# Row maxima by an operation that also copies the scores: a threshold attention with a gated MLP on one core

## The chip, the cores and the metric

The kernel runs on one core of a Trainium2 chip. The metric is device time in microseconds; smaller is better. TensorE (PE) multiplies and writes PSUM; VectorE (DVE) and ScalarE (ACT) read PSUM and SBUF; GpSimd (POOL) reads SBUF only; SyncE (SP) issues most of the transfers. Each engine works through its own instructions strictly in the order in which they stand, and waits on semaphores for the others.

## The reference

The inputs are q, k and v of 8 batches, 8 heads, 576 rows and 64 columns, a threshold `tau` of 0.02, and the weights of a gated MLP.

```python
scale = 1.0 / np.sqrt(q.shape[-1])
scores = scale * np.matmul(q, k.transpose(0, 1, 3, 2))
thresh = np.max(scores, axis=-1, keepdims=True) - tau
scores = np.where(scores >= thresh, scores, -1000000000.0)
scores = scores - np.max(scores, axis=-1, keepdims=True)
attn = np.exp(scores)
attn = attn / (np.sum(attn, axis=-1, keepdims=True) + 1e-09)
x = np.matmul(attn, v)                       # heads side by side: (8, 576, 512)

h = np.maximum(x @ w_in, 0.0)                # 512 -> 1024
u, v = h[..., :512], h[..., 512:]
v_n = (v - mean(v)) / np.sqrt(var(v) + 1e-06)
v_s = np.einsum('ts,bsd->btd', w_spatial, v_n) + b_spatial[None, :, None]
out = (u * v_s) @ w_out
```

So every row of scores needs its maximum before anything else can be done with it: only the scores within `tau` of it survive, and those are weighted by their exponentials.

## The kernel before, in words

The heads are taken in pairs, 32 of them. A step `g` is 128 query rows of a pair against all 576 keys, 144 steps in all, 18 to a batch. Its scores, 576 columns for each of the two heads, lie in one of two PSUM buffers of three banks (`s_ring`), at columns 96 and 864, so that both heads share the middle bank.

A step runs as follows, with the letters by which the lists name its parts:

- `S`, `G`, `Y`: PE computes the scores (line 816). `G` is an empty instruction on some other engine that keeps two matmuls from the shared bank at one time.
- `M` (`top`, line 850): VectorE takes the maxima of both heads in one reduction over 1152 columns and writes their negatives into the shared bank of the same PSUM buffer.
- `B` (`shift`, line 856): VectorE makes of the two numbers the bias `negm` (threshold minus maximum), a tiny operation.
- `E`, `F` (`spread`, lines 871 and 874): ScalarE reads the scores of one head from PSUM and writes them, shifted, to SBUF, into one of three buffers `e`. After `F` the PSUM buffer is free for step g+2.
- A step is of one of two kinds (table `WAYS`, the same in both kernels). In the 96 steps of kind `a`, ScalarE's `E` and `F` are a leaky rectifier that drives all scores under the threshold far down, and `Z` (line 909) takes the exponential of 1152 columns into the half-precision buffer `p`. In the 48 of kind `n`, `E` and `F` take the exponential at once, in half precision, and VectorE makes a mask of it (`C`, line 893) and applies it (`A`, line 902).
- `T`: a transfer turns `p` into `pT`. `P`, `i`, `p`: PE multiplies by v with a column of ones, VectorE takes the reciprocals of the sums (line 531) and scales (line 534).

The MLP of a batch runs one to two batches behind its attention: `v`/`bv`, `n`, `k`, `bs`, `ba`, `N` (second half of the first product, its statistics and normalization), `u`/`eu` (first half), `s`/`es` (product with the spatial weights, then the gate on VectorE, line 752), `o`/`eo` (the output). `Q..`/`q..`/`kd` turn q and k on PE. The evictions from PSUM run on ScalarE, or with a `d` before their name on VectorE.

What runs when is written out by hand as `ORDER`, a list of such names for each of the eight batches, and `LAST`, for what follows: the numbers behind a colon say by how many batches a part lags. The program issues the parts in the order of the list, and each engine takes its own from that.

Of the kernel before, what the change touches and what calls it, by code (L numbers as in the profile page):

```python
# [34 lines left out]
(  # L35
# [18 lines left out]
(  # L54
# [130 lines left out]
def kernel(  # L185
# [17 lines left out]
    nc = tc.nc  # L203
# [592 lines left out]
    def on_act(g):  # L796

        return way(g) in "anrs"
# [445 lines left out]
```

## Time and profile before

| what | value |
|---|---|
| three timed runs | 436.28, 437.15 and 436.65 us, median 436.65 |
| profiled execution | span 433.6 us, first to last instruction; the page has no other time for it, and the median is 3.0 us above the span |
| TensorE clock granted | 1.00 |
| matmul / weight load busy | 407.3 us (94%) / 253.7 us (58%) |
| VectorE busy | 374.6 us (86%), 681 instructions |
| ScalarE busy | 383.9 us (89%), 587 instructions |
| GpSimd busy | 167.5 us (39%) |
| 144 row maxima (line 850) | 196.1 us of VectorE, from 7.5 us to 396.4 us (their starts) |
| 288 `E` and `F` (lines 871, 874) | 66.8 + 133.1 us of ScalarE |

A busy time is the time in which at least one instruction of the engine was in work; rows of one engine can overlap a little. A row of the groups reads: line, engine, operation, output and input with their shapes, count, busy time, mean of one in ns, then the idle time in front of them and what ended it. A row of the engines in order of time begins with its start and its length in us. A row of the stretches has the stretch, its length, and then the busy time of PE, weight load, VectorE, ScalarE and GpSimd in it.

### The profile page before, as it was taken

The numbers are of one execution on the slowest core, as the hardware profiler recorded it, in microseconds if no ns is written. First come the engines' busy times: TensorE is split into PE (matmuls) and PEld (weight loads), VectorE is DVE, ScalarE is ACT, GpSimd is POOL, SyncE is SP. The second block draws the span as 40 slices with busy tenths as digits, with TensorE's granted clock in tenths as the row PEclk, the third lists the DMA queues.
The fourth block names the chain that finished last, engine by engine and source line by source line (L and its number), as shares of the span: only waits on it lengthen the run. The fifth ranks groups of instructions, "written<-read, shape, count | busy, mean of one in ns | idle before, by whom it ended". The sixth has DMA issues, their size and how long they took to land.

```text
span 433.6 us, 12917 instructions
## 1 busy us (share of the span) xinstructions
PE 407.3 (94%) x5028; PEld 253.7 (58%) x5028; DVE 374.6 (86%) x681; ACT 383.9 (89%) x587; POOL 167.5 (39%) x374
## 2 busy tenths in 40 slices
PE   7678879989999999998999999999999999999995
PEld 4446655565755666574665656555666656564642
DVE  6999989898989889987889988988999999998652
ACT  4999989999999988998988999999999989999262
POOL 1253525682335611545143713356114630264020
PEclk9999999999999999999999999999999999999999
DMA  7999999999899998999979999999999999889923
GB/s 195 224 237 232 246 247 221 194 212 197 226 241 212 246 208 183 218 184 178 254 139 250 216 159 248 233 209 205 232 209 232 181 232 194 172 124 193 164 68 118
DMA packets 224700, 88.15 MB, mean 203 GB/s; under 512 B 195648, under 2 KB 220352, under 8 KB 224640
## 3 DMA queue, kind: packets, MB, share of 16 engines
q1 hardware_dynamic: 224192, 86.75, 99.7%
q8 instruction: 39, 0.64, 0.6%
q10 hardware_dynamic: 368, 0.33, 0.2%
q0 software_dynamic: 80, 0.26, 0.2%
q14 instruction: 21, 0.17, 0.2%
HBM read 32.79 MB, written 9.44 MB: 97 GB/s over the span
## 4 chain that ended last, share of the span: by engine, by line
PE 64%; ACT 13%; DVE 8%; DMA 6%; issue 4%; POOL 3%; SPq 0%; ACTq 0%; DVEq 0%; POOLq 0%
PE s L816 26%; ACT e L874 6%; PE f L738 6%; DVE s L850 5%; PE f L496 5%; PE f L709 5%; PE f L434 4%; PE f L642 4%; PE f L767 4%; DMA pT<-p 3%; ACT p L909 2%; DMA xT<-xn 2%; ACT e L871 2%; PE f L491 2%; PE f L627 1%
## 5 line engine op out<-in xcount | busy, mean ns | idle before, releaser
L850 DVE TENSOR_REDUCE s<-s 128x2 f32<-128x1152 f32 x144 | 196.1, 1362 | 21.3 <-PE s L816 18.0
L816 PE MATMUL s<-qkT 64*64 64x160 f32 (+1 forms) x2304 | 171.4, 415 | 12.6 <-ACT e L874 6.6
L816 PEld LDWEIGHTS s<-qkT 64*64 64x64 f32 x2304 | 106.5, 131 | 71.3 <-ACT e L874 18.8
L874 ACT ACTIVATE e<-s,negm 128x576 f32<-128x576 f32 x192 | 133.1, 744 | 9.6 <-DVE negm L856 7.0
L909 ACT ACTIVATE p<-e 128x1152 f16<-128x1152 f32 x96 | 111.6, 1173 | 0.7 <-PE s L816 0.2
L871 ACT ACTIVATE e<-s,negm 128x576 f16<-128x576 f32 x96 | 66.8, 746 | 5.0 <-DVE negm L856 2.9
L320 POOL CAST v<-vl 128x512 bf16<-128x512 f32 x32 | 20.2, 631 | 77.0 <-PE s L816 65.7
L496 PE MATMUL f<-v,pT 128*128 128x65 bf16 x984 | 44.4, 194 | 0.0
L496 PEld LDWEIGHTS <-pT 128*128 128x128 f16 x1024 | 41.8, 98 | 2.2 <-issue 0.2
L293 POOL COPY qn<-ql 128x512 f32<-128x512 f32 x31 | 20.4, 659 | 49.9 <-PE s L816 47.5
L902 DVE TENSOR_TENSOR p<-e 128x576 int32<-128x576 int32 x48 | 37.2, 778 | 0.4 <-PE s L816 0.2
L738 PE MATMUL f<-wsT,vn 128*128 128x512 bf16 x135 | 33.0, 380 | 0.0
L491 PE MATMUL f<-v,pT 128*128 128x130 bf16 x123 | 27.3, 222 | 3.6 <-DMA pT<-p 3.5
L709 PE MATMUL f<-xT,w_in 128*128 128x512 bf16 x116 | 29.7, 380 | 0.5 <-ACT qkT L414 0.3
L694 POOL TENSOR_SCALAR vn<-vrel,rs,nm 128x512 bf16<-128x512 f32 (+1 forms) x35 | 28.1, 801 | 3.6
L642 PE MATMUL f<-w_in,xT 128*128 128x512 bf16 x112 | 27.9, 380 | 0.3 <-DMA xT<-xn 0.3
L446 POOL COPY qkT<-qkT 64x64 f32<-64x64 f32 x32 | 9.5, 296 | 44.8 <-PE s L816 17.6
L534 DVE TENSOR_TENSOR xn<-f,r 128x384 bf16<-128x384 f32 x46 | 24.9, 551 | 1.3 <-PE s L816 0.8
L856 DVE TENSOR_SCALAR negm<-s 128x2 f32<-128x2 f32 x144 | 22.2, 154 | 4.0 <-PE s L816 1.5
L767 PE MATMUL f<-w_o,gT 128*128 128x512 bf16 x100 | 25.4, 379 | 0.1
L893 DVE TENSOR_SCALAR e<-e 128x1152 uint16<-128x1152 f16 x48 | 23.0, 478 | 0.1
L687 POOL TENSOR_TENSOR rs<-rs,mhalf 128x1 f32<-128x1 f32 (+1 forms) x35 | 21.2, 607 | 2.9
(171 smaller groups left out, 531.4 us busy)
## 6 DMA issues: line engine op xcount, KB each, us to landing
vl<-in_v_dram SPq DMA_DIRECT2D x16, 512.0 KB, 5.3
ql<-in_q_dram SPq DMA_DIRECT2D x15, 512.0 KB, 4.6
kl<-in_k_dram SPq DMA_DIRECT2D x15, 512.0 KB, 5.3
out_dram<-oo SPq DMA_DIRECT2D x12, 512.0 KB, 3.7
pT<-p SPq DMA_TRANSPOSE x141, 4.6
uT<-in_moe_w_in_dram SPq DMA_DIRECT2D x3, 512.0 KB, 5.1
uT<-in_moe_w_spatial_dram SPq DMA_DIRECT2D x2, 576.0 KB, 4.4
vx<-in_v_dram SPq DMA_DIRECT2D x16, 64.0 KB, 4.3
```

What stands on the lines that cost most here:

```text
L491: nc.tensor.matmul(out=t[:, at:at + 130], lhsT=pt[:, 4, rows], rhs=vt[:, 4:6, :].rearrange("p b d -> p (b d)"), start=True, stop=False)
L496: nc.tensor.matmul(out=t[:, at + 65 * h:at + 65 * h + 65], lhsT=pt[:, 5 * h + j, rows], rhs=vt[:, 6 * h + j, :], start=False, stop=(h == 1 ...
L642: nc.tensor.matmul(out=t, lhsT=x_of(b, f, slice(c * P, (c + 1) * P)), rhs=w_in[:, f, 512:1024], start=(f == 0), stop=(f == 3))
L709: nc.tensor.matmul(out=t, lhsT=w_in[:, m, f * P:(f + 1) * P], rhs=x_of(b, m, slice(0, 512)), start=(m == 0), stop=(m == 3))
L738: nc.tensor.matmul(out=t, lhsT=vn[:, c, f * P:(f + 1) * P], rhs=wsT[:, c, 0:512], start=(c == 0), stop=(c == 4))
L767: nc.tensor.matmul(out=t[:n], lhsT=gs[b][:, f, c * P:c * P + n], rhs=w_o[:, f, :], start=(f == 0), stop=(f == 3))
L816: made.append(nc.tensor.matmul(out=s_ring[g % 2][halves[k], at[h] + lo:at[h] + hi], lhsT=qks[n][halves[h], 0, m:m + 64], rhs=qks[n][halves ...
L850: nc.vector.tensor_reduce(out=nm[:, heads], in_=view(s_ring[g % 2], at[h0], dims), axis=AX.X, op=ALU.max, negate=True)
L871: nc.scalar.activation(out=half_e(g)[0][:, S * h:S * h + S], in_=s, func=ACT.Exp, bias=bias_, scale=scale if steps[g][1] == 4 else 1.0)
L874: nc.scalar.activation(out=e, in_=s, func=ACT.Prelu, bias=bias_, scale=scale if steps[g][1] == 4 else 1.0, alpha=1e30)
L902: nc.vector.tensor_tensor(out=numerators(g).bitcast(I32), in0=e.bitcast(I32), in1=kept.bitcast(I32), op=ALU.bitwise_and)
L909: nc.scalar.activation(out=numerators(g), in_=e_ring[g % 3].rearrange("p h s -> p (h s)"), func=ACT.Exp)
```

## The change

`M` becomes two operations, one for each head. Each reads 576 scores from PSUM, adds a column of zeros that is read 576 times over, writes the sum, which is the scores themselves, into the step's `e` buffer in SBUF, and keeps the largest of them, which goes to a small tile `peak` in SBUF. `B` reads `peak`, with the sign turned, since the old reduction gave the negative. `E` and `F` read the `e` buffer and write into the same buffer, in place. In the steps of kind `n`, where they write half precision, the result of a head lies in the first half of that head's own row, and the mask in its second half; the views in `C` and `A` become three-dimensional for that. A column `zero` is filled once. All eight lists and the first two of `LAST` are new, with no count of any part changed; some evictions have changed between VectorE and ScalarE.

```diff
@@ ORDER, one list of eight @@
-    "S0:0 G0:0 Y0:0 s0:2 OUT3:3 eu0:2 A15:1 E17:1 sq2:0 F17:1 S1:0 T13:1 M0:0 G1:0 Y1:0 s1:2 Z16:1 C17:1 L6:0 "
...
+    "S0:0 A15:1 aG0:0 Y0:0 QR1:0 M17:1 P100:1 P101:1 F16:1 qr1:0 E16:1 Z16:1 M0:0 P102:1 s0:2 i10:1 S1:0 "
...
+    zero = const.tile([P, 1], F32, name="zero")
...
-    negm = {}
+    negm, peak = {}, {}
 
     def top(g, heads=slice(0, 2)):
 
-        if on_act(g):
-            nm = s_ring[g % 2][:, 704:706]
-        elif g in negm:
-            nm = negm[g]
-        else:
-            nm = negm[g] = small.tile([P, 2], F32, name="negm")
-        h0, n = heads.start, heads.stop - heads.start
-        dims = [[at[1] - at[0], n], [1, S]] if n > 1 else [[1, S]]
-        nc.vector.tensor_reduce(out=nm[:, heads], in_=view(s_ring[g % 2], at[h0], dims), axis=AX.X,
-                                op=ALU.max, negate=True)
+        if g not in peak:
+            peak[g] = small.tile([P, 2], F32, name="peak")
+        for h in range(heads.start, heads.stop):
+            nc.vector.tensor_tensor_reduce(
+                out=e_ring[g % 3][:, h, :], in0=view(s_ring[g % 2], at[h], [[1, S]]),
+                in1=zero.broadcast_to([P, S]), scale=1.0, scalar=float("-inf"),
+                op0=ALU.add, op1=ALU.max, accum_out=peak[g][:, h:h + 1])
 
     def shift(g):
 
         nm = negm[g] = small.tile([P, 2], F32, name="negm")
-        nc.vector.tensor_scalar(out=nm, in0=s_ring[g % 2][:, 704:706],
-                                scalar1=scale if steps[g][1] == 4 else 1.0,
+        nc.vector.tensor_scalar(out=nm, in0=peak[g],
+                                scalar1=-(scale if steps[g][1] == 4 else 1.0),
                                 scalar2=float(tau) + (0.0 if way(g) == "a" else half_step),
                                 op0=ALU.mult, op1=ALU.add)
 
     def half_e(g):
 
-        t = e_ring[g % 3].rearrange("p h s -> p (h s)").bitcast(F16)
-        return t[:, 0:1152], t[:, 1152:2304]
+        t = e_ring[g % 3].bitcast(F16)
+        return t[:, :, 0:S], t[:, :, S:2 * S]
 
     def spread(g, h):
 
-        s = view(s_ring[g % 2], at[h], [[1, S]])
+        s = e_ring[g % 3][:, h, :]
...
+        nc.vector.memset(zero, 0.0)
```

What this makes of the instructions on each engine is shown at three places. First VectorE, inside a batch in the middle of the run, where nearly all of its work is of this kind. (`s_94` and `s_95` are the two PSUM buffers; `e_103` to `e_105`, after the change `e_104` to `e_106`, the three SBUF buffers; the names in brackets are the semaphores that an instruction waits for, by the engine or transfer that raises them.) Before:

```order
L850 TENSOR_REDUCE s_94<-s_94 128x2 [waits PE_49,Activation_49]
L902 TENSOR_TENSOR p_113<-e_105 128x576 [waits DMAHW3_49,DVE_49]
L856 TENSOR_SCALAR negm<-s_94 128x2 [waits DVE_49]
L850 TENSOR_REDUCE s_95<-s_95 128x2 [waits PE_49,Activation_49]
L893 TENSOR_SCALAR e_104<-e_104 128x1152
L856 TENSOR_SCALAR negm<-s_95 128x2 [waits DVE_49]
L902 TENSOR_TENSOR p_115<-e_104 128x576 [waits DMAHW1_49,DVE_49]
```

and with the change, two steps as well:

```order
L848 ISA e_105,peak<-s_94,zero 128x576 [waits PE_49,Activation_49]
L848 ISA peak 128x1
L848 ISA e_105,peak<-s_94,zero 128x576
L848 ISA peak 128x1
L856 TENSOR_SCALAR negm<-peak 128x2 [waits DVE_49]
L848 ISA e_106,peak<-s_95,zero 128x576 [waits PE_49]
L848 ISA peak 128x1
L848 ISA e_106,peak<-s_95,zero 128x576
L848 ISA peak 128x1
L755 TENSOR_TENSOR gT<-f,uT 128x512 [waits PE_49]
L856 TENSOR_SCALAR negm<-peak 128x2 [waits DVE_49]
```

One reduction has become four instructions: for each head the main one and a second, of one column, that puts out `peak`. The first of them now also writes `e`, and the wait for ScalarE (`Activation`) there is for the step that used this `e` buffer before.

Second TensorE, at the scores of one step in the same batch. Before:

```order
L816 MATMUL s_95<-qkT 64x160 [waits Activation_49]
L816 MATMUL s_95<-qkT 64x160
L816 MATMUL s_95<-qkT 64x416 x4
L816 MATMUL s_95<-qkT 64x160 [waits Pool_sequencer_49]
L816 MATMUL s_95<-qkT 64x160
```

and with the change:

```order
L819 MATMUL s_94<-qkT 64x160 [waits DVE_49]
L819 MATMUL s_94<-qkT 64x160
L819 MATMUL s_94<-qkT 64x416 x4
L819 MATMUL s_94<-qkT 64x160 [waits Pool_sequencer_49]
L819 MATMUL s_94<-qkT 64x160
```

The matmuls are the same. The first of them waited for ScalarE to give the PSUM buffer back and now waits for VectorE.

Third ScalarE in the same batch. Before:

```order
L874 ACTIVATE e_103<-s_94,negm 128x576 [waits DVE_49,Activation_49]
L874 ACTIVATE e_103<-s_94,negm 128x576
L412 ACTIVATE uT<-f 128x512 [waits PE_49]
L874 ACTIVATE e_104<-s_95,negm 128x576 [waits DVE_49]
L874 ACTIVATE e_104<-s_95,negm 128x576
L909 ACTIVATE p_111<-e_105 128x1152 [waits DMAHW1_49]
```

and with the change:

```order
L874 ACTIVATE e_105<-e_105,negm 128x576 [waits DVE_49]
L874 ACTIVATE e_105<-e_105,negm 128x576
L874 ACTIVATE e_106<-e_106,negm 128x576 [waits DVE_49]
L909 ACTIVATE p_111<-e_105 128x1152 [waits DMAHW2_49,Activation_49]
L874 ACTIVATE e_106<-e_106,negm 128x576
L657 ACTIVATE vrel<-f 128x512 [waits PE_49]
```

The two activations of a step now read the buffer that they write.

More of the change, by code (lines that the diff above doesn't have):

```diff
@@ L20 @@
 ORDER = [(
[14 rows of a table removed]
-(
[18 rows of a table removed]
-(
[18 rows of a table removed]
-(
[17 rows of a table removed]
-(
[17 rows of a table removed]
-(
[17 rows of a table removed]
-(
[17 rows of a table removed]
-(
[16 rows of a table removed]
[12 rows of a table added]
+(
[19 rows of a table added]
+(
[17 rows of a table added]
+(
[18 rows of a table added]
+(
[17 rows of a table added]
+(
[18 rows of a table added]
+(
[17 rows of a table added]
+(
[16 rows of a table added]
 LAST = [(
-    "C15:1 es1:2 OUT3:3 A15:1 E17:1 T13:1 s3:2 "),
-(
[3 rows of a table removed]
+    "u3:2 eu3:2 E15:1 s0:2 s1:2 es0:2 T11:1 T9:1 C15:1 T12:1 T7:1 OUT4:3 A15:1 T13:1 E17:1 s3:2 es1:2 OUT3:3 "
+    "F17:1 "),
+(
[4 rows of a table added]
 (
@@ L861, in half_e @@
     def half_e(g):
-        t = e_ring[g % 3].rearrange("p h s -> p (h s)").bitcast(F16)
-        return t[:, 0:1152], t[:, 1152:2304]
+        t = e_ring[g % 3].bitcast(F16)
+        return t[:, :, 0:S], t[:, :, S:2 * S]
     def spread(g, h):
-        s = view(s_ring[g % 2], at[h], [[1, S]])
+        s = e_ring[g % 3][:, h, :]
         e, bias_ = e_ring[g % 3][:, h, :], negm[g][:, h:h + 1]
         if way(g) in "nrs":
-            nc.scalar.activation(out=half_e(g)[0][:, S * h:S * h + S], in_=s, func=ACT.Exp,
+            nc.scalar.activation(out=half_e(g)[0][:, h, :], in_=s, func=ACT.Exp,
                                  bias=bias_, scale=scale if steps[g][1] == 4 else 1.0)
@@ L901, in pick @@
         if way(g) == "n":
-            nc.vector.tensor_tensor(out=numerators(g).bitcast(I32), in0=e.bitcast(I32),
+            nc.vector.tensor_tensor(out=numerators(g).rearrange("p (h s) -> p h s", h=2).bitcast(I32), in0=e.bitcast(I32),
                                     in1=kept.bitcast(I32), op=ALU.bitwise_and)
         else:
-            nc.gpsimd.tensor_tensor(out=numerators(g), in0=e, in1=kept, op=ALU.mult)
+            nc.gpsimd.tensor_tensor(out=numerators(g).rearrange("p (h s) -> p h s", h=2), in0=e, in1=kept, op=ALU.mult)
     def exps(g):
```

273 rows, old and new, of tables (LAST, ORDER) are left out of this document.

## Prediction

> **What bounds the kernel now.** I read the page's first part, then its chain, then the stretches, then the groups by form, and last the engines in order of time. The page says that TensorE is the fullest, but that two others stand close behind it:
>
> ```profile
> PE 407.3 (94%) x5028; PEld 253.7 (58%) x5028; DVE 374.6 (86%) x681; ACT 383.9 (89%) x587; POOL 167.5 (39%) x374
> PE 64%; ACT 13%; DVE 8%; DMA 6%; issue 4%; POOL 3%; SPq 0%; ACTq 0%; DVEq 0%; POOLq 0%
> ```
>
> Those are means over unlike stages. The row maxima run from 7.5 us to the end of the last one at 397.8 us; the view of stretches, cut there and at 60 us (columns: PE, weight load, DVE, ACT, POOL, then clock and DMA), gives
>
> ```profile
> 7.50:60.00 52.50, 40.53 (x591) 28.02 (x589) 49.05 (x77) 49.25 (x71) 19.98 (x42) 1.00 1.15 232
> 60.00:397.80 337.80, 330.16 (x4091) 206.16 (x4092) 302.45 (x533) 316.14 (x483) 142.68 (x319) 1.00 1.04 208
> 110.00:397.80 287.80, 283.69 (x3522) 176.60 (x3519) 258.88 (x457) 269.68 (x411) 115.62 (x262) 1.00 1.03 206
> 397.80:433.60 35.80, 30.73 (x316) 16.68 (x314) 18.98 (x49) 15.93 (x30) 3.31 (x5) 1.00 0.55 125
> ```
>
> The reader is to see two regimes. In the ramp (first row) there is hardly any gMLP work for TensorE yet: PE is busy 77% of it, VectorE 93.4% and ScalarE 93.8%, so there those two set the pace. From 60 us on PE takes over: 97.7% there, 98.6% from 110 us, with VectorE at 90% and ScalarE at 94%. The granted clock is 1.00 in every row. In the last 35.8 us no row maximum is left, and the order of instructions after the last scores has the same rows on PE in both kernels, so I leave that tail as it is.
>
> What PE waits for at the scores, and what VectorE waits for there, the view of waits says (us in total, times, longest):
>
> ```profile
> DVE s L850 <- PE s L816: 18.0, 43, 0.9
> PE s L816 <- ACT e L874: 6.6, 13, 0.9
> PE s L816 <- ACT e L871: 3.9, 10, 0.7
> ```
>
> PE itself loses 6.6 + 3.9 = 10.5 us because a PSUM buffer of scores is given back only when ScalarE has read it. This is what the change takes away; more than 10.5 us cannot come of that directly.
>
> **The change, part by part.** First VectorE. The rows that price it, from the groups by form:
>
> ```profile
> L850 DVE TENSOR_REDUCE s<-s 128x2 f32<-128x1152 f32 x144 | 196.1, 1362 | 21.3 <-PE s L816 18.0 <-PE f L496 0.8 <-ACT vrel L654 0.6
> L856 DVE TENSOR_SCALAR negm<-s 128x2 f32<-128x2 f32 x144 | 22.2, 154 | 4.0 <-PE s L816 1.5
> L752 DVE TENSOR_TENSOR gT<-f,uT 128x512 bf16<-128x512 f32 x27 | 18.4, 685 | 2.1 <-PE s L816 1.4 <-PE f L738 0.4
> L534 DVE TENSOR_TENSOR xn<-f,r 128x384 bf16<-128x384 f32 x46 | 24.9, 551 | 1.3 <-PE s L816 0.8
> ```
>
> A two-input operation with one input in PSUM takes 551 ns for 384 columns and 685 for 512, so (685 - 551)/128 = 1.05 ns a column, and 685 + 64 x 1.05 = 752 ns for the 576 columns of one head. Rows overlap, though, and what counts is from start to start. VectorE in order of time:
>
> ```profile
> 100.16 0.16 DVE L856 TENSOR_SCALAR negm<-s 128x2 f32<-128x2 f32 x1
> 100.24 0.68 DVE L752 TENSOR_TENSOR gT<-f,uT 128x512 bf16<-128x512 f32 x1
> 100.84 0.28 DVE L410 COPY qkT<-f 128x128 f32<-128x128 f32 x1
> 106.05 1.37 DVE L850 TENSOR_REDUCE s<-s 128x2 f32<-128x1152 f32 x1 [0.62 <-PE s L816]
> 107.32 0.75 DVE L902 TENSOR_TENSOR p<-e 128x576 int32<-128x576 int32 x1
> ```
>
> The product starts 0.08 us after the tiny operation in front of it, the copy 0.60 after a 0.68 us product, and the 1.37 us reduction holds the engine 1.27 us. So a new main operation holds it 0.752 - 0.08 = 0.67 us. Two of them stand in a step in place of one reduction. But the order shows a second instruction behind each, of 128x1, that carries the peak: 288 more. Trace before has no such row on VectorE. Its nearest rows are the 0.16 us `negm` (0.08 from start to start) and ScalarE's own read of an accumulator:
>
> ```profile
> 224.21 0.25 ACT L651 ACTIVATION_READ_ACCUMULATOR vrel<-f 128x1 f32 x1
> 224.30 1.42 ACT L874 ACTIVATE e<-s,negm 128x576 f32<-128x576 f32 x2
> 226.16 0.26 ACT L675 ACTIVATION_READ_ACCUMULATOR sq<-vrel,nmean 128x1 f32 x1
> 226.25 0.64 ACT L416 COPY oo<-f 128x512 f32<-128x512 f32 x1
> ```
>
> ScalarE's next operation starts 0.09 us after the read, so I take 0.08 us for VectorE's. Bounds: nothing below (the read wholly inside the main operation's drain), 0.154 us above with the main operation's full 0.752 in front of it (no overlap at all). A step costs VectorE 2 x 0.67 + 2 x 0.08 = 1.50 us in place of 1.27: **+0.23 us**, 33.1 us over 144 steps; by the bounds +0.07 (10 us) and 2 x 0.906 - 1.27 = +0.54 (78 us). `B` stays one operation behind it, and the mask and the choice (48 steps) keep their element counts; they cost nothing new. The lists move evictions: VectorE sheds 5 output copies, 1 uT and 1 qkT of 512 columns, 3 copies of 128 and 2 of 256, and gains 2 of pT and 3 of xT before the last maximum; with 0.60 us held for 512 columns (as above), 0.28 - 0.08 = 0.20 for 128 and, an estimate between the two, 0.34 for the others that is -4.2 - 0.6 - 0.7 + 1.7 = -3.8 us.
>
> Second, ScalarE. `E` and `F`, 288 of them, now read SBUF:
>
> ```profile
> L874 ACT ACTIVATE e<-s,negm 128x576 f32<-128x576 f32 x192 | 133.1, 744 | 9.6 <-DVE negm L856 7.0 <-PE s L816 0.9 <-DVE st L661 0.2
> L675 ACT ACTIVATE sq<-vrel,nmean 128x512 bf16<-128x512 f32 x6 | 4.4, 730 | 0.0
> L416 ACT COPY qkT<-f 128x512 f32<-128x512 f32 x24 | 14.2, 593 | 1.1 <-PE f L434 1.0
> L416 ACT COPY qkT<-f 128x128 f32<-128x128 f32 x20 | 5.3, 265 | 1.4 <-PE f L453 0.8
> L909 ACT ACTIVATE p<-e 128x1152 f16<-128x1152 f32 x96 | 111.6, 1173 | 0.7 <-PE s L816 0.2
> ```
>
> The square is the trace's activation from SBUF with a bias of its own: 730 ns for 512 columns. At (593 - 265)/384 = 0.85 ns a column it would take 784 for 576, against 744 from PSUM: +0.04 us x 288 = 11.5 us, of which 2 x 23 x 0.04 = 1.8 for the ramp's 23 steps. Bounds are nothing (the source makes no difference) and twice that. The evictions it takes over come to 2 us. No DMA and no matmul is added; the memory set of the zero column is one tiny row at the start.
>
> Third, the waits. PE's wait for scores' buffer now ends with VectorE's two operations, not with ScalarE: the hold of a buffer shrinks by the shift and two activations. In exchange VectorE fills one of three `e` buffers as its first act and so waits until ScalarE (or VectorE's own choice) is done with step g-3. Behind a VectorE that waits there stand, in its queue, the sums and products of attention output, the gates and the statistics, and PE waits for those. From maximum to freed buffer it takes 1.50 + 0.16 for the shift, 1.42 for the two activations (the row at 224.30) and 1.17 for the exponential, 4.3 us with nothing between, while three steps last 3 x 390.3/144 = 8.1 us: covered, as long as ScalarE is no more than some 3.8 us late.
>
> **The sum**, for the span of the profiled execution, 433.6 us. The three timed runs have a median of 436.65, which is 3.0 more; I add that at the end. Steps by stretch, from the view of stretches for L850 alone:
>
> ```profile
> 7.50:60.00 52.50, 31.31 (x23) 1.00 1.15 232
> 60.00:397.80 337.80, 164.78 (x121) 1.00 1.04 208
> ```
>
> Ramp: VectorE's 49.05 + 23 x 0.23 = 54.3 us does not fit into 52.5. At the share it had there (93.4%) the ramp becomes 58.2, at the 98.6% that PE shows later 55.1: +2.6 to +5.7, I take **+4**. PE has 12 us free there, so nothing else hides it. Rest: VectorE 302.45 + 121 x 0.23 - 3.8 = 326.5, ScalarE 316.14 + 242 x 0.04 + 2 = 327.8, PE 330.16 unchanged, all in 337.8: 96.7%, 97.0%, 97.7%. None overflows, so the 28 us that VectorE gains there are hidden under PE; but its reserve falls from 35 to 11 us, and with three engines above 96% I allow **+1.5** for collisions. In all 433.6 + 5.5 = 439.1, and with 3.0 about **442 us**; its own range is 438 to 448.
>
> One rule of the Trainium skill speaks against the change. Vector Engine (DVE) Microarchitecture Reference, Points that are easy to get wrong, says that a scalar-tensor-tensor form with two SBUF sources that aren't bf16 runs at half rate, since both read ports are taken and none is left for the accumulator. Here one source is PSUM and the other a zero column from SBUF, and the rows L752 and L534, of another form without an accumulator, run at 1.05 ns a column; the sum goes by those.
>
> **The rivals.**
>
> *Faster, by the freed PSUM.* VectorE's 18.0 us of waits for scores and PE's 10.5 us for ScalarE are both ends of one tight ring, which the change loosens. If VectorE then reaches 98.6% in the ramp (+2.6) and PE 99.5% in the rest (330.16/0.995 = 331.8, -6.0), the sum is -3.4: 433. With the read of the accumulator hidden too, the ramp loses its +2.6 and it is 431. For it: PE's waits are real and the ring is shorter. Against: in the ramp VectorE's work alone is longer than the stretch, and afterwards only 7.6 us of PE's idle time is left to win, with VectorE's reserve nearly gone.
>
> *Slower, by the in-order VectorE queue.* The `e` ring ties VectorE to ScalarE, and each stall holds evictions that PE needs. If the busiest of the three then reaches no more in the rest than the 93.8% of the ramp, where two were close to full, it takes 330.16/0.938 = 352 us: +14, with the ramp's +5.7 that is 456. It decides once ScalarE runs some 3.8 us behind. For it: three engines at 97%. Against: PE reached 98.6% beside a ScalarE at 94%.
>
> *Slower, by a dearer operation.* If the main operation must end before its accumulator is read, a step costs 2 x (0.752 + 0.08) - 1.27 = +0.39: the rest has 302.45 + 47.2 - 3.8 = 345.9 us of VectorE, at 97% 356.6, +19, the ramp (49.05 + 9)/0.934 = 62.1, +10: 465. With no overlap at all (+0.54) by the same two quotients about 487. If the main operations ran at half rate, 576 x 1.05 = 0.6 us more each, 144 x 1.2 = 173 us would be added: above 600. Nothing in these rows points to that last one.
>
> It is what the rule of the Trainium skill named above would give.
>
> *Nothing.* The ramp pays +4 and the ring gives 4 back: 436 to 437.5.
>
> **How the numbers follow.** Likeliest 0.43 (all of it slower); faster by the ring 0.24; nothing 0.10; slower by the queue 0.12; a dearer operation 0.11, of it half rate 0.02. What a measurement of this kernel tells from no change is about 0.2%. Faster is thus 0.24, the same 0.10, slower 0.43 + 0.12 + 0.11 = 0.66. The range leaves out the lower end of the fast case, the upper end of the queue's and the dearer operation: 432 to 457.
>
> **What would show it.** Right: 288 main rows near 750 ns, their reads starting some 0.67 us after them and holding the engine under 0.1 us; `E` and `F` near 784; PE's waits for ScalarE at the scores gone; the 23rd maximum ending some 4 us later than now; VectorE near 97% afterwards. Wrong: main rows far from 750, a read that starts only when its main row ends, PE above 99% from 60 us on, or VectorE idle on ScalarE for more than some 10 us, which would mean that the `e` ring has become the tight one.

## The result

The changed kernel takes 441.13 us, median of 6 runs (439.91 to 442.38), against 436.6 us for the kernel before in the same series: a ratio of 1.012, 95% interval 1.0087 to 1.0154. It is slower by about 5 us. The ratios here leave out single executions that lie over 1.5% above the fastest one of their kernel, while the medians are over all executions. The forecast was 442 us. That the total fits is in good part luck: the places where the time went were mostly not the ones that the forecast named, and the rest of this document is about that.

The first part of the page of the changed kernel, its span being 439.6 us and its own time 441.35 us, with the clock's row (40 slices, tenths of full speed):

```profile
PE 419.4 (95%) x5028; PEld 238.0 (54%) x5028; DVE 387.8 (88%) x1107; ACT 393.5 (90%) x594; POOL 166.7 (38%) x374
PEclk9989999999999999999999999999999899999999
```

TensorE works 12.1 us longer than before (407.3 us) and the span grew by 6.0, so PE now idles less. Its groups, those of the new operation, of the shift `B`, of the scores and of `E` and `F` in the steps of kind `a` (columns: busy us, mean ns of one | idle before):

```profile
L848 DVE CUSTOM_DVE_ANT_0 e<-s,zero 128x576 f32<-128x576 f32 x288 | 204.9, 751 | 14.6 <-PE s L819 9.9 <-ACT p L909 2.6 <-ACT vrel L657 0.2
L848 DVE DVE_READ_ACCUMULATOR2_ANT peak<- 128x1 f32 x288 | 23.4, 81 | 0.0
L856 DVE TENSOR_SCALAR negm<-peak 128x2 f32<-128x2 f32 x144 | 32.3, 229 | 0.6
L819 PE MATMUL s<-qkT 64*64 64x160 f32 (+1 forms) x2304 | 185.8, 419 | 8.4 <-DVE peak L848 4.5 <-POOLq L834 2.9 <-POOL qkT L449 0.8
L874 ACT ACTIVATE e<-e,negm 128x576 f32<-128x576 f32 x192 | 139.9, 769 | 4.6 <-DVE negm L856 3.9
```

The row of the scores in the kernel before:

```profile
L816 PE MATMUL s<-qkT 64*64 64x160 f32 (+1 forms) x2304 | 171.4, 415 | 12.6 <-ACT e L874 6.6 <-ACT e L871 3.9 <-DVE negm L856 1.5
```

Four things are to be seen. PE's 10.5 us of waiting for ScalarE at the scores are gone, as the change says. A new single wait of 2.9 us for GpSimd's queue (`POOLq`) has come. The scores take PE 185.8 us in place of 171.4, with the same 2304 matmuls. And `B`, of which only the source and the sign have changed, has gone from 154 to 229 ns.

The stretches, in the columns of the forecast (PE, weight load, DVE, ACT, POOL, clock, DMA; the 0.97 of the first is a dip of the clock from 23.25 to 26.66 us):

```profile
7.50:60.00 52.50, 47.52 (x615) 28.63 (x610) 50.27 (x146) 49.17 (x71) 18.60 (x39) 0.97 1.05 223
60.00:406.00 346.00, 336.98 (x4085) 190.13 (x4082) 315.23 (x893) 326.56 (x491) 143.23 (x322) 1.00 1.02 205
```

To see where the time was lost, I set the starts of the row maxima of the two kernels beside each other, from VectorE's timeline (us from the start of the span; step 143 is the last):

```
step             18     27     54     81    108    117    126    143
before         48.2   73.0  149.3  225.1  301.4  325.0  350.3  396.4
changed        49.4   72.6  150.0  225.4  302.5  328.0  356.9  403.7
difference     +1.2   -0.4   +0.7   +0.3   +1.1   +3.0   +6.6   +7.3
```

Up to step 108 the change costs 1 us. Between steps 108 and 126 it loses 5.5, and in the last stretch, after the last maximum, about 1.3 come back (span +6.0). So there is one place to look at first; there 1.9 us are lost ahead of step 117 and 3.9 between 117 and 120.

GpSimd in order of time, there (start, us; the bracket is the idle time before and what ended it):

```profile
332.46 0.19 POOL L685 TENSOR_SCALAR rs<-mv 128x1 f32<-128x1 f32 x1 [10.13 <-DVE mv L668]
...
336.71 1.13 POOL L296 COPY kn<-kl 128x512 f32<-128x512 f32 x1
337.80 0.61 POOL L323 CAST v<-vl 128x512 bf16<-128x512 f32 x1
338.36 0.52 POOL L329 CAST v<-vx 64x64 bf16<-64x64 f32 x2
338.95 0.62 POOL L323 CAST v<-vl 128x512 bf16<-128x512 f32 x1
339.51 0.53 POOL L329 CAST v<-vx 64x64 bf16<-64x64 f32 x2
```

TensorE at the same time, and the stretch behind it:

```profile
339.67 1.26 PE L819 MATMUL s<-qkT 64*64 64x160 f32 x16 [2.87 <-POOLq L834]
```

```profile
340.50:344.00 3.50, 3.50 (x29) 1.34 (x25) 2.47 (x8) 1.09 (x2) 0.22 (x1) 0.53 0.98 220
```

GpSimd had waited 10.13 us for a mean and variance from VectorE, and then worked off its backlog of copies without a pause. The relay `G` of step 120, an empty instruction that lets PE go on to the rest of that step's scores, stood in GpSimd's queue behind them. PE stood still for 2.87 us, and 1.0 us after it had started again its granted clock fell to half for 3.4 us (0.53 over the second row): 1.7 us of PE's work more. VectorE ran dry for 2.25 us and ScalarE for 3.54 in turn.

### The profile page after: what moved, and what is told of

The parts are those of the page before. It is cut to its first block, busy times and chain, and to the rows that moved or that the text cites. A ratio compares the mean times of both kernels' runs of the same rounds, so it can differ in the third digit from the quotient of the medians.

```text
span 439.6 us, 13268 instructions
## 1 busy us (share of the span) xinstructions
PE 419.4 (95%) x5028; PEld 238.0 (54%) x5028; DVE 387.8 (88%) x1107; ACT 393.5 (90%) x594; POOL 166.7 (38%) x374
## 4 chain that ended last, share of the span: by engine, by line
PE 68%; ACT 13%; DVE 9%; issue 4%; DMA 2%; POOL 2%; SPq 1%; ACTq 0%; POOLq 0%; DVEq 0%
PE s L819 26%; PE f L741 6%; PE f L499 6%; PE f L437 5%; DVE e L848 4%; PE f L645 4%; ACT e L874 4%; PE f L770 4%; PE f L712 4%; ACT e L871 3%; ACT p L909 3%; DMA pT<-p 2%; PE f L494 2%; PE f L630 2%; DVE negm L856 1%
## 5 line engine op out<-in xcount | busy, mean ns | idle before, releaser
L848 DVE CUSTOM_DVE_ANT_0 e<-s,zero 128x576 f32<-128x576 f32 x288 | 204.9, 751 | 14.6 <-PE s L819 9.9
L819 PE MATMUL s<-qkT 64*64 64x160 f32 (+1 forms) x2304 | 185.8, 419 | 8.4 <-DVE peak L848 4.5
L874 ACT ACTIVATE e<-e,negm 128x576 f32<-128x576 f32 x192 | 139.9, 769 | 4.6 <-DVE negm L856 3.9
L819 PEld LDWEIGHTS s<-qkT 64*64 64x64 f32 x2304 | 90.6, 133 | 58.9 <-issue 28.2
L871 ACT ACTIVATE e<-e,negm 128x576 f16<-128x576 f32 x96 | 70.5, 770 | 4.4 <-DVE negm L856 4.3
L902 DVE TENSOR_TENSOR p<-e 128x576 int32<-128x576 int32 x48 | 38.3, 800 | 0.2
L741 PE MATMUL f<-wsT,vn 128*128 128x512 bf16 x135 | 33.1, 379 | 0.9 <-ACT qkT L419 0.9
L856 DVE TENSOR_SCALAR negm<-peak 128x2 f32<-128x2 f32 x144 | 32.3, 229 | 0.6
L449 POOL COPY qkT<-qkT 64x64 f32<-64x64 f32 x32 | 8.1, 255 | 64.6 <-ACT qkT L419 35.8
L419 ACT COPY qkT<-f 128x512 f32<-128x512 f32 (+1 forms) x48 | 20.3, 423 | 4.8 <-PE f L437 2.3
```

Of the source, the lines that this page charges most:

```text
L741: nc.tensor.matmul(out=t, lhsT=vn[:, c, f * P:(f + 1) * P], rhs=wsT[:, c, 0:512], start=(c == 0), stop=(c == 4))
L819: made.append(nc.tensor.matmul(out=s_ring[g % 2][halves[k], at[h] + lo:at[h] + hi], lhsT=qks[n][halves[h], 0, m:m + 64], rhs=qks[n][halves ...
L848: nc.vector.tensor_tensor_reduce(out=e_ring[g % 3][:, h, :], in0=view(s_ring[g % 2], at[h], [[1, S]]), in1=zero.broadcast_to([P, S]), scal ...
L856: nc.vector.tensor_scalar(out=nm, in0=peak[g], scalar1=-(scale if steps[g][1] == 4 else 1.0), scalar2=float(tau) + (0.0 if way(g) == "a" e ...
L871: nc.scalar.activation(out=half_e(g)[0][:, h, :], in_=s, func=ACT.Exp, bias=bias_, scale=scale if steps[g][1] == 4 else 1.0)
L874: nc.scalar.activation(out=e, in_=s, func=ACT.Prelu, bias=bias_, scale=scale if steps[g][1] == 4 else 1.0, alpha=1e30)
```

## The experiments

In the experiments' files the lists are packed more tightly, so the line numbers are lower: in the rows below the scores are L688 or L689, the new operation L718 or L719, the old reduction L722, `B` L726 or L727, `E` and `F` L744, the relay L704, `Z` L779. A token such as `G12:0` names the part `G`, its step in the batch and how many batches back it belongs.

Times are medians, ratios are against the kernel before on the same chip, with 95% intervals.

### The operation under the old order

First: is the new order of the lists a part of the change's price, or does the operation need it? The lists of before put `Z` (or `C` and `A`) of a step behind the maximum three steps later 34 times, which the ring of three `e` buffers doesn't allow any more. With those 34 moves, the same in all three kernels, there is a control and two forms of the change.

```diff
-  T9:0 M16:0 Z13:0 QR0:-1
+  T9:0 Z13:0 M16:0 QR0:-1
```

The control, before with the 34 moves and nothing else:

> A control for the two runs with the old lists: the kernel before, with the same 34 moves of Z, or C and A, and nothing else. If the wait of VectorE for ScalarE on the e ring made the 59 us there: 435 to 440. If the moves themselves did, since Z now stands in front of other work on ScalarE: 470 to 495.

The whole change of the operations under those lists:

> The whole change to the operations with the lists of the kernel before (same 34 moves): scores copied, ScalarE works in place, PSUM freed by VectorE. Theory 1: no better than the changed kernel, 440 to 443, since VectorE and ScalarE carry the same work. Theory 2: the early release gives back up to 10.5 us of PE's waits for ScalarE, of which I expect a third, against 7 us more of ScalarE's work: 432 to 436, so the new lists cost 5 us or more.

And the same, with `E` and `F` reading PSUM as before (the copy is written and not used):

> The new maximum alone: two copying operations per step, but ScalarE still reads the scores from PSUM, so a PSUM buffer is freed as late as before; lists of the kernel before, with Z, or C and A, of 34 steps moved up to stand before the maximum that reuses their e buffer. The copy is made and then overwritten. Theory 1 (the prediction's: the work added to VectorE sets the loss): VectorE gets 144 x 0.07 = 10 us more, 23 x 0.07 = 1.6 us of it in the ramp where nothing hides it, and waits for ScalarE on the e ring: 438.5 to 442. Theory 2 (the new lists make the loss, the operation is hidden): 436 to 438.

Measured: 441.28 us, 1.0146 (1.0091 to 1.0202), for the control; 496.83 us, 1.1417 (1.1373 to 1.1462), with the change; 494.37 us, 1.1367 (1.1325 to 1.141), with PSUM as the source. The moves cost 6 us, the operation under this order 53 to 56. The waits on VectorE, of the kernel with the whole change and of the control:

```profile
DVE e L718 <- ACT p L779: 57.3, 30, 3.5
ACT e L744 <- DVE negm L726: 33.1, 35, 2.8
```

```profile
DVE s L722 <- PE s L688: 19.7, 46, 1.0
```

The expectations for the two kernels with the operation, 432 to 443 us, were missed by over 50. VectorE's maximum stands 57.3 us waiting for ScalarE's exponential, 30 times, where the control waits for PE's scores, and ScalarE in turn 33.1 us for the shift. That is the forecast's rival of the in-order queue: the `e` ring has become the tight one. A part goes through the clock, which was granted at 0.973 in the mean of these runs and at 0.998 in the control's. What decides it is the order of the work and not the source of `E` and `F`: the two kernels differ by 2.5 us with overlapping intervals. Under the new lists the same wait is 2.6 us (the L848 row above). So the lists are what makes the operation affordable; with them the rival does not happen.

### Scores that start earlier

In the new lists the scores of 86 of 144 steps are begun (`S`) and finished (`Y`) with other PE work between (83 by the matmuls in the trace); before, none were. I closed that gap in three ways: by moving `S` and `G` down to `Y`, by moving `G` and `Y` up to `S`, and by moving `Y` alone up to a relay that had fired early anyway.

```diff
-  Y4:0 S5:0 es2:2 B3:0 M4:0 ... p11:1 B4:0 G5:0 E3:0 ... X0:1 Y5:0 S6:0
+  Y4:0 es2:2 B3:0 M4:0 ... p11:1 B4:0 E3:0 ... X0:1 S5:0 G5:0 Y5:0
```

> The changed kernel with the start of each step's scores (and its turn of the bank) moved down to its end, so that all sixteen matmuls of a step stand together on PE, as they did before; in the changed kernel other PE work stands between them in 86 steps. If the breaks cost PE what its busy time says (185.8 against 171.4 us): 430 to 437. If the ends in the trace are only modelled so: 440 to 443. If the early start of the scores is what keeps VectorE fed: 444 or more.

Measured: 465.01 us, 1.0687 (1.063 to 1.0743). The wait on VectorE:

```profile
DVE e L718 <- PE s L689: 35.4, 44, 5.2
```

VectorE waits 35.4 us for scores, in place of 9.9. So the early start feeds VectorE, and here that is worth more than what the broken scores take out of PE's time, as the third case of the expectation had it.

Up instead of down (from the kernel with one relay moved, told below):

```diff
-  Y4:0 S5:0 es2:2 B3:0 M4:0 ... p11:1 B4:0 G5:0 E3:0 ... X0:1 Y5:0 S6:0
+  Y4:0 S5:0 G5:0 Y5:0 es2:2 B3:0 M4:0 ... p11:1 B4:0 E3:0 ... X0:1 S6:0
```

> The relay kernel with the last part of each step's scores, and the turn of the bank, moved up behind the first part wherever the list allows it (120 steps), so that PE does sixteen matmuls in one go and early. Theory S: the breaks cost PE 0.41 us each, 7 us in all; if the turn of the bank comes in time on the other engines' queues, 430 to 436, if those are late PE waits in front of the last part: 440 or more. Theory V: VectorE paces, no gain: 437 to 440.

Measured: 445.49 us, 1.0248 (1.0189 to 1.0307), 7.5 us more than its base (437.98). Its waits:

```profile
PEld s L689 <- DVE peak L718: 12.9, 22, 1.6
DVE e L718 <- ACT p L779: 10.3, 13, 2.3
```

PE's weight loads now wait for the maxima (12.9 us, 5.7 in the base), and VectorE, pushed ahead, for ScalarE. By these rows the work between the two parts of the scores was cover for those waits.

### What VectorE's work is worth

The forecast rests on this: 0.23 us more of VectorE in each step, hardly any of it hidden in the ramp, most of it afterwards. Two kernels change VectorE's work, both from the kernel with one relay moved. One takes the maximum by a single reduction without the copy, from step 3 on, and lets ScalarE read a constant tile in SBUF; it leaves out the copy of the scores, and with it VectorE's wait for the `e` buffer (2.3 us in the base), so it is not a change of work alone. The other puts a copy of two columns behind each of the 288 main operations.

```diff
-        for h in range(heads.start, heads.stop):
-            nc.vector.tensor_tensor_reduce(out=e_ring[g % 3][:, h, :], ...)
+        nc.vector.tensor_reduce(out=peak[g], in_=view(s_ring[g % 2], ...), ...)
...
-        s = e_ring[g % 3][:, h, :]
+        s = e_ring[g % 3][:, h, :] if g < 3 else fixed
```

```diff
             nc.vector.tensor_tensor_reduce(out=e_ring[g % 3][:, h, :], ...)
+            nc.vector.tensor_copy(out=spare[2 * (g % 3) + h], in_=mhalf.broadcast_to([P, 2]))
```

> The relay kernel with a cheaper maximum: from the fourth step on one reduction over both heads, without the copy; ScalarE reads a constant tile in SBUF in its place, so the output is not the reference's. It takes 144 x 0.07 = 10 us off VectorE, and VectorE's wait for the e buffer with it. Theory V (VectorE's work paces the ramp and is felt afterwards): 432 to 436. Theory S (VectorE's extra work is hidden, the rest of the loss lies in PE's broken scores): 436.5 to 439.

> The relay kernel with a dearer maximum: a copy of 128x2 into a spare tile behind each of the two operations, 0.08 us each by the row of the tiny operations, 0.16 us a step, which is the cost per step that the prediction had (0.23 against 0.07 as measured). Theory V: 23 x 0.16 = 3.7 us in the ramp and 1 to 3 after it: 441 to 446. Theory S: 437 to 440.

Measured: 435.02 us, 0.9996 (0.9957 to 1.0036), for the cheaper maximum, 3 us under its base of 437.98, 1.0059, which ran on another chip (the kernel before took 435.48 us beside the base and 435.38 here); 445.23 us, 1.0252 (1.0186 to 1.0318), for the dearer one, 7 us over it. VectorE's work is felt in both directions. The row of the added copies, then VectorE in order of time, and the stretch from 7.5 to 76 us of the dearer kernel and of its base:

```profile
L723 DVE COPY spare<-mhalf 128x2 f32<-128x2 f32 x288 | 61.9, 215 | 0.0
```

```profile
182.37 0.16 DVE L723 COPY spare<-mhalf 128x2 f32<-128x2 f32 x1
182.44 0.74 DVE L719 CUSTOM_DVE_ANT_0 e<-s,zero 128x576 f32<-128x576 f32 x1
```

```profile
7.50:76.00 68.50, 59.85 (x733) 35.39 (x732) 67.86 (x233) 61.71 (x87) 25.97 (x51) 0.98 1.01 222
```

```profile
7.50:76.00 68.50, 62.01 (x762) 36.58 (x760) 65.16 (x190) 64.37 (x94) 27.12 (x53) 0.98 1.07 226
```

A copy holds VectorE 0.07 us where nothing disturbs it, but 0.13 on the average of the 281 that are followed at once, so the addition was 0.26 us a step and not the 0.16 meant. 45 of the 288 last over 0.25 us, each ending with an operation of GpSimd; the section on the shift comes back to that. In these 68.5 us VectorE is then 99% busy (67.86), against 95% in the base. By the starts of the maxima the dearer kernel is 4.0 us behind its base at step 27, 5.1 at step 54 and 8.4 at step 143. That is the forecast's picture, VectorE's work paid for in the ramp and mostly hidden later, at a price a step that the change itself does not have.

### The one late relay

```diff
-  sv3:0 sv1:0 G12:0 s4:2 F8:0
+  sv3:0 sv1:0 vG12:0 s4:2 F8:0
```

The relay of step 120 goes into VectorE's queue instead of GpSimd's; nothing else is changed.

> The changed kernel with one empty instruction moved: the one that turns the shared bank of step 120 goes from GpSimd's queue to VectorE's. Theory 2: GpSimd's queue, ten us behind for a statistic of VectorE, held PE there, 2.9 us idle at 337 to 339.7 and some work after it: 436.5 to 439. Theory 1: VectorE has no reserve and the loss reappears elsewhere: 440.5 to 442.

Measured: 437.98 us, 1.0059 (1.0028 to 1.0091). To see that the stall is no accident of one execution, the changed kernel was run once more, beside a kernel that moves the relays of steps 5 and 6 as well, whose lateness PE had waited for in the ramp:

```diff
-  S5:0 sv1:0 G5:0 Y5:0 M4:0 QA2:0 S6:0 G6:0
+  S5:0 sv1:0 vG5:0 Y5:0 M4:0 QA2:0 S6:0 vG6:0
```

> The changed kernel once more, beside the runs of the next kernel, so that the relay's share is a comparison on one chip. Theory Q (the one late relay of step 120 on GpSimd's queue is a property of the lists and comes back in every run): about 441 us, 1.010 to 1.015 of before, and in its profile PE again waits over 2 us for GpSimd's sequencer at the scores of step 120, at about 340 us. Theory R (it was an accident of the one profiled run): no such wait in this profile, and a time near that of the kernel with the relay moved, 438 us.

> The kernel with the relay of step 120 moved, and the relays of steps 5 and 6 moved from GpSimd's to VectorE's queue as well: in the profile of the kernel with one relay moved PE waited 1.33 us for GpSimd's sequencer at 17.8 us and 1.92 us for VectorE's maximum at 25.4 us. If a relay that comes late in the first 30 us is paid for in full, 435 to 436.5 us (1.3 to 2.5 us less than with one relay moved, 437.98); if GpSimd's lateness there is only the next wait's cover (VectorE or the loads being late just behind it), 437.5 to 438.5 us.

Measured: 440.69 us, 1.012 (1.0083 to 1.0157), and 437.48 us, 1.0067 (1.0036 to 1.0099). The row of the changed kernel's second profile:

```profile
338.72 1.59 PE L819 MATMUL s<-qkT 64*64 64x160 f32 x16 [2.89 <-POOLq L834]
```

The stall is there again, 2.89 us in place of 2.87, and the clock was at half from 339.4 to 342.8 us, as it was from 340.7 to 344.1 in the first. With the relay moved, steps 108 to 126 take 50.4 us in place of 54.4 (48.9 before): the 1.9 us ahead of step 117 stay. By the times of this series, with the two early relays moved as well, it is 3.2 us of the change's 5.6. Those two are worth nothing that shows, 437.48 against 437.98, or 1.0067 against 1.0059: PE waits there for the next thing instead (1.0 us for a transposition's source, 1.15 for a maximum).

### The shift that reads SBUF

There remain 0.6%, with the relay moved. `B` had grown in the profile after, and its long rows have company. VectorE, then GpSimd, in the changed kernel:

```profile
67.64 0.99 DVE L856 TENSOR_SCALAR negm<-peak 128x2 f32<-128x2 f32 x1
```

```profile
67.48 1.12 POOL L372 CAST wsb<-uT 128x512 bf16<-128x512 f32 x1
68.53 0.24 POOL L375 CAST wsb<-uT 128x64 bf16<-128x64 f32 x1
```

An operation on 128x2 elements lasts 0.99 us, and it ends 0.03 us after GpSimd's cast. Of the 144 rows of `B` 23 are above 0.25 us, from 0.27 to 1.11: 19 stand beside a copy or cast of GpSimd and 4 beside its scaling `vn`, and each ends some 0.02 us after that operation. Before, where `B` read PSUM, there were none. In the mean `B` holds VectorE 0.17 us from start to start, where it held it 0.08. The Trainium skill has a rule for it: SBUF — State Buffer, Who interferes with whom, says that a scalar operation of VectorE can take both pairs of SBUF ports, the second of which it shares with GpSimd, and that whoever comes first keeps that pair for its whole instruction. To test it I gave `B` a source and a destination that can't be halved alike:

```diff
-        nm = negm[g] = small.tile([P, 2], F32, name="negm")
-        nc.vector.tensor_scalar(out=nm, in0=peak[g], ...)
+        six = small.tile([P, 6], F32, name="negm")
+        nm = negm[g] = six[:, 0:2]
+        nc.vector.tensor_scalar(out=six, in0=view(peak[g], 0, [[0, 3], [1, 2]]), ...)
```

> The kernel with one relay moved, in which the shift B reads its two maxima three times over (rows of 2, read 3 times, written to one row of 6; the first two are used): the same small operation on VectorE, with 4 more elements. In the changed kernel 23 of the 144 B rows took 0.33 to 1.0 us, each beside a copy of GpSimd, where the kernel before, whose B read PSUM, had none above 0.25 us; from start to start a B held VectorE 0.173 us against 0.083. Theory P (B now reads and writes SBUF, takes both of VectorE's SBUF ports and waits for GpSimd's copy to let go of one): with a source of 3 rows and a destination of one row of 6 it cannot split its elements between two ports. The Trainium skill, VectorE: DVE Perf Modes, What auto-detection actually checks, asks for outermost dimensions that are both even or equal. Then no B row above 0.25 us, mean 155 to 175 ns in place of 214, and some 10 to 13 us less of VectorE's time; by the cheaper maximum, which took 11 us from VectorE and 3 us from the time, 434.5 to 436.5 us, 0.998 to 1.002 of before. Theory Q (SBUF as a source is slow for so short an operation, or the long rows have another cause): long rows as before, mean above 200 ns, 438 us.

Measured: 435.81 us, 1.0006 (0.9975 to 1.0038). The row of `B`, in this kernel and in its base:

```profile
L727 DVE TENSOR_SCALAR negm<-peak 128x6 f32<-128x6 f32 x144 | 20.6, 147 | 0.6
```

```profile
L726 DVE TENSOR_SCALAR negm<-peak 128x2 f32<-128x2 f32 x144 | 30.2, 214 | 0.6
```

With three times the elements the mean is 147 ns, not one row is above 0.25 us, and the hold is 0.08 us as before the change. Theory P of the expectation holds, and the skill's rule with it. With the relay and `B` mended, the changed kernel is as fast as the kernel before, as far as an interval of 0.3% either way can tell. So the two are worth the whole loss. That is a net sum: the new operations still hold VectorE 0.09 us a step longer, and what makes up for that was not taken apart. The granted clock of their runs averages 0.995 here, 0.994 in the base and 0.996 in the kernel before.

One last kernel tried to get more out of that one, by closing the scores where the relay has time to spare:

```diff
-  p11:1 B4:0 G5:0 E3:0 ... X0:1 Y5:0 S6:0
+  p11:1 B4:0 G5:0 Y5:0 E3:0 ... X0:1 S6:0
```

> The kernel with one relay moved and B reading three rows, in which the last matmuls of a step's scores (Y) are moved up right behind the relay G in the 47 steps where in that kernel's profile the relay had fired over 0.5 us before the first twelve matmuls ended: other PE work then lies between the two parts of the scores in 61 steps in place of 83; the other engines keep their order. Theory B (a break costs PE 0.41 us, as 12 matmuls last as long as 16, and PE is the bound from 60 us on): PE's work falls by 22 x 0.41 = 9 us, of which at most the share that PE sets comes out, since VectorE stands at 90% and ScalarE at 95% of their time there: 432 to 434.5 us, 0.990 to 0.997 of before. Theory C (the lists are balanced: the work that is pushed behind Y by 0.42 us feeds ScalarE and VectorE, and the relays come late once PE is earlier): no gain or a loss, 435.5 to 440 us, with PE waiting over 2 us more for VectorE or the relays at the scores.

Measured: 438.3 us, 1.0037 (1.0006 to 1.0069). No gain, as Theory C had it, and Theory B's sum was wrong. PE's time for scores depends on the length of each unbroken run of them, from its start to the next instruction's: 4 matmuls 0.421 us, 12 1.120, 16 1.133, 20 1.391, 28 2.090, 32 2.103. A `Y` that is moved up from the next step's `S` breaks a run of 20 there while it mends one here. By those durations the new lists' scores come to 170.4 us in this kernel's base, 171.5 here and 161.0 in the kernel before (one run of 24 counted as 28). Whether it is slower than its base is not shown: the medians are 2.5 us apart, the ratios 0.3%, with overlapping intervals.

## Why the forecast was right, and where it was not

The direction and the size came out, the reasons for them in the main did not. Of the +4 us in the ramp nothing came, and behind it, where the forecast had +1.5, 5.5 us went between steps 108 and 126 alone. The span was 439.6 us for 439.1 forecast; the 3.0 us added from span to time are 1.75 to 1.82 in the runs of the changed kernel. That these add up to the right total is luck.

**The operation.** 751 ns for 752, and 0.679 us from start to start for 0.67: right. The half rate of the Trainium skill's rule (Vector Engine (DVE) Microarchitecture Reference, Points that are easy to get wrong), which is stated for two sources in SBUF, did not come: with one source in PSUM it is 1.2 ns a column, start to start.

**The accumulator's read.** Mis-sized: 0.08 us was taken for each, and it costs nothing. VectorE's timeline in the changed kernel:

```profile
328.69 0.08 DVE L848 DVE_READ_ACCUMULATOR2_ANT peak<- 128x1 f32 x1
328.69 0.75 DVE L848 CUSTOM_DVE_ANT_0 e<-s,zero 128x576 f32<-128x576 f32 x1
329.36 0.08 DVE L848 DVE_READ_ACCUMULATOR2_ANT peak<- 128x1 f32 x1
329.36 0.18 DVE L668 BATCH_NORM_AGGREGATE mv<-st 128x2 f32<-128x6 f32 x1
```

The read and whatever follows it start together; the median over some 240 such places is 0. The lower bound of the forecast was the truth, and the step's operations cost 2 x 0.679 - 1.271 = +0.09 us. The nearest row taken, ScalarE's read, was another engine's.

**"`B` stays one operation behind it", at no cost.** This is the step of VectorE's price that was wrong. Its source moved from PSUM to SBUF, and that alone made it wait for GpSimd: +0.09 us a step in this profile (+0.06 in the second). Together VectorE's price is +0.15 to +0.18 us a step in place of +0.23, so that the price was near for two errors of opposite sign. The experiment on `B` shows that it matters: 1.0059 to 1.0006.

**ScalarE.** `E` and `F` are 769 ns for 784 forecast: +25 ns for SBUF as a source and not +40, 7 us in all. Under the old lists the source made 2.5 us of difference, within the intervals.

**The ramp, +4.** It didn't come: the maximum of step 27 starts 0.4 us earlier than before. In the row of 7.50 to 60.00 VectorE has 50.27 us of work, 95.8%, not the 54.3 that would not fit. The mechanism is right, as the dearer kernel shows (4.0 us behind at step 27, VectorE at 99%). But the smaller price alone would not have made it fit: 49.05 + 23 x 0.15 = 52.5 is the whole stretch. The stretch for the new operation alone and for `B` alone, and in the kernel before for `B` alone (VectorE's work stands behind the length):

```profile
7.50:60.00 52.50, 32.58 (x91) 0.97 1.05 223
7.50:60.00 52.50, 5.42 (x22) 0.97 1.05 223
7.50:60.00 52.50, 3.45 (x22) 1.00 1.15 232
```

With the 31.31 us of the old reduction these two have grown by 3.2 us, and VectorE's whole work by 1.2. The other 2.0 us it was spared elsewhere, 0.9 of it by evictions: six of 3.5 us in the stretch before, four of them of 512 columns of `qkT`, are now seven smaller ones of 2.6. The forecast counted what the lists move off VectorE, -3.8 us, wholly behind the ramp.

**The rest, +1.5 for collisions.** The allowance stood in the right place, with the wrong thing in mind: one collision alone, GpSimd's backlog before a relay, took some 3 us with the dip of the clock behind it. Nothing in the trace of before could show it, since that relay stands behind the copies only in the new lists (`sv3:0 sv1:0 G12:0`); there it could be read. That "the matmuls are the same", PE 330.16 us "unchanged", failed too: broken runs add 9.4 us of scores. In the total they don't show, as the kernel with both repairs has them still; by this account they stand in the place of the 10.5 us that PE waited for ScalarE before.

**The rivals.** The in-order queue is real, and 53 to 56 us large, under the old order; the new order keeps it at 2.6 us. The dearer operation and the half rate are refuted by the 0.679 us. The faster case, by the freed PSUM, is not borne out: even with the cheaper maximum, which has all of the new lists and the early buffers, the time is that of before (0.9996). That kernel still has the slow `B`, with 21 rows above 0.25 us; the cheaper maximum and the mended `B` together were not run, and might be faster. The freed buffers gave the lists their early scores, and by the sums above these cost PE about as much as they save it; that is argued, not tested.

**What was to show it.** Main rows, reads and PE's lost waits for ScalarE came as said. "VectorE near 97% afterwards" did not: 315.23 of 346 us, 91%, mainly since its price was lower.

## What to carry to other kernels

When an operation's operand moves from PSUM to SBUF, price every small instruction that reads it again, and look at what GpSimd does beside it: 0.16 us became up to 1.1. An empty relay on a queue of long copies is only as punctual as the queue (PE waited 2.9 us for it here), so put it where nothing can pile up ahead of it. And a freed wait is worth only what the next limit leaves: here 10.5 us of PE's waiting went and 9.4 us of broken matmul runs came.

## What the runs showed of the hardware

- The read of VectorE's accumulator, an 81 ns row, costs nothing from start to start: what follows begins with it at some 240 places.
- A VectorE operation of 2 elements a partition, SBUF to SBUF, lasted up to 1.11 us beside a GpSimd cast; of 6, with rows of 2 read three times into one row, never above 0.25.
- 12 matmuls of scores take as long as 16 (1.120 and 1.133 us), as if the last four, of 160 columns, ran beside others; alone they take 0.421 us.
- The granted clock halves for 3.4 us behind some of PE's idle stretches: 0.7 to 1.0 us behind the 2.87 and 2.89 us of idling near 339 us in the two profiles of the changed kernel, and in the ramp behind 1.14 us that end at 23.15 us in the first and 1.92 us that end at 25.23 us in the second. Others of 1 to 2 us, such as the 1.84 us that end at 157.7 us, had no such dip, so the rule for it stays open. The Trainium skill (TensorE: Matmul & The Clock Gate, What's actually happening) has the clock set by a free-running window of about 3.4 us and halved after an idle one; the length of the dips, 3.41 us, agrees, but here 2.87 us of idling and less were enough. Over the second series' runs the mean clock was 0.992 in the changed kernel and 0.997 in the one before, so a part of the 5 us may go through the clock.
